# One head's tokens on all 128 partitions: a linear-attention and mixture-of-experts kernel with a new token layout

## The chip, the cores and the metric

The kernel runs on one core of a Trainium2 chip. The metric is the device time of one launch in microseconds (us). Three runs of the kernel before took 371.85, 367.94 and 371.0 us, median 371.0.

## The reference, cut to what matters

Linear attention (a cosine-weighted one) is followed by a top-1 mixture of experts on its output. All inputs are float32.

```
q, k, v: (B=8, H=8, S=576, D=64)
q_p, k_p = phi(x) = [relu(x)*cos(theta), relu(x)*sin(theta)]   # theta = pi/2 * position / S
kv  = einsum('bhsf,bhsd->bhfd', k_p, v);  z = sum_s k_p
num = q_p @ kv;  den = q_p . z + 1e-6;  x = num / den          # 4608 tokens of 512
logits = x @ w_gate;  expert = argmax(logits);  gate = softmax(logits)[expert]
out[i] = gate[i] * (relu(x[i] @ w1[expert]) @ w2[expert])      # 8 experts, 512 -> 1024 -> 512, capacity 1152
```

## The kernel before, in words

**Order of the work.** Every piece of work is registered with a planner (class `Plan`, lines 59 to 179): engine, cost in us, dependencies, buffers, a priority that the table `PHI` (line 28) shifts by kind. `schedule` runs a list schedule over these costs, and `emit` issues the instructions in the order of planned start. So each engine's queue is a fixed list; costs and `PHI` set its order, and on the chip each engine works through its list and waits at semaphores.

**Attention, batch by batch (8 batches).** Partition p holds head parity o = p // 64 and token group p % 64; each token group has 9 consecutive tokens j. A head therefore lies on 64 partitions, and two heads share the 128.

- `load` (L420 to L438): six DMAs a batch on SP's queue (v, k, v, k, q, q), 576 KB each, one DMA over all 128 partitions; a partition receives two runs of 9\*64 floats (2304 bytes).
- `scale_k`, `scale_v` (L448 to L467): per token j, k becomes relu(k)\*cos and a copy v\*tan is made, each 128x256 per instruction (128x128 in batch 0, split in two): 18 instructions a batch, on ACT or DVE as the planner chooses.
- `q_relu` (L480, tag reluq): one DVE instruction of 128x1152 per half batch, also reordering q; then `q_part` (L487): 9 TensorE transposes of 128x128 per half batch (L493) and three evictions from PSUM (L500).
- `kv_half` (L524, matmul at L535): k as stationary 64x64, v and v\*tan as moving 64x132; 9 j, two column halves c, two row halves o. The four combinations (o, c) are four 64x64 quarters of the array.
- Small steps that fold `w_gate` into kv: copy (L548), transpose (T, L559), product (G, L573), copy back (L579).
- `p_unit` (L595): num and den and logits of 128 tokens and four heads, 10 units a batch: four matmuls of 64 rows (L603), ACT copy (L613), DVE multiply-add (L617). Units rotate through three PSUM slots.

**Routing (L635 to L819).** DVE computes argmax, gate, and with small matmuls (`f_cnt`, L716) each token's rank within its expert; POOL scatters the token rows to a DRAM buffer `xd` sorted by expert (L796).

**Experts.** 43 blocks of 128 sorted rows (`block`, L969): fetch on SP's queue (L994) into one of four `xr` buffers, transpose (L1003), copy (L1007), up-projection in two halves m=0 and m=1 against w1 (L1023), relu (L1032/1034), transpose (L1041), copy (L1047), down-projection (L1067), copy (L1072), indirect store by POOL (L1081). The first 20 blocks ("a") can start when six batches are routed; the other 23 ("b") need all batches and the zero rows `s_pad` (L924 to L933), which fill each expert's last block: eight DMAs of 128.5 KB issued from ACT's queue.

**Weights.** POOL's queue loads w1 and w2 with a cast to bf16. w1's first half (w1a, L945) has its own place and loads between batches 4 and 7; the second half (w1b) and w2's first half live in a pool that takes the place of all attention buffers, so their loads wait for the operation `swap` (L1124), after the last attention batch; w2's second half takes w1a's place.

Of the kernel before, what the change touches and what calls it, by code (L numbers as in the profile page):

```python
# [20 lines left out]
P = 128  # L21
# [7 lines left out]
    "G": 0.31, "KV": 0.33, "P": 0.35, "Q": -0.14, "T": -0.36, "carry": 1.34, "count": -1.01, "down": 0.6,  # L29
    "end": -3.84, "fetch": 0.26, "gout": 1.98, "ix": 1.87, "kva": 0.07, "load": -0.87, "pad": -0.91,  # L30
    "pre": -0.09, "relu": -1.78, "reluq": -0.77, "rq": 8.8, "scat": -0.24, "seen": -0.1, "tab": 0.69,
    "tmp": 1.28, "tsb": 1.62, "turn": -1.07, "up": -0.52, "vt": 17.49, "w1": 1.81, "w2": 0.68, "warm": -0.07,
    "wg": -0.36, "xT": -5.44, "xturn": -10.62,
# [3 lines left out]
class Slots:  # L37


    def __init__(self, name, n, fifo=True):  # L40
        self.name, self.n, self.fifo = name, n, fifo
        self.holder = [None] * n
        self.vers, self.given = [], 0

# [14 lines left out]
class Plan:  # L59
# [30 lines left out]
    def schedule(self, window=0.25, switch=0.15, sticky=0.6):  # L90
# [11 lines left out]
        while done < len(self.ops):  # L102
            best = {}
            cands = []
            for o in ready:
                t = o.avail
                ok = True
                for v in o.vers:
                    if v.slot is not None:
                        t = max(t, v.ready)  # L110
                    else:
                        ts = []
                        for h in v.slots.holder:
                            if h is None:
                                ts.append(0.0)
                            elif all(u.start is not None for u in h.uses):
                                ts.append(max(u.end for u in h.uses))
                        if not ts or (v.slots.fifo and v.turn != v.slots.given):
                            ok = False
                            break  # L120
                        t = max(t, min(ts))
# [23 lines left out]
            for v in o.vers:  # L145
                if v.slot is None:
                    opts = []
                    for i, h in enumerate(v.slots.holder):
                        if h is None:
# [11 lines left out]
            if o.dma:  # L161
                dma_free = max(dma_free, o.end) + o.dma
                o.end = dma_free + 1.6
# [19 lines left out]
def kernel(  # L183
# [21 lines left out]
    assert J == 9  # L205
    NJ = J // 2
# [12 lines left out]
    U0, U1, U2 = 4, 41, 42  # L219
# [36 lines left out]
    qrS = Slots("qr", 2)  # L256
# [5 lines left out]
    xrS = Slots("xr", 4)  # L262
# [4 lines left out]
    VH = J * D + 2  # L267
    VX = D + 2
    v_t = [early.tile([P, HB * VH + HB * J * VX], FP32, name=f"v{i}") for i in range(vS.n)]

    def v_raw(slot):
        return v_t[slot][:, 0:HB * VH].rearrange("p (h x) -> p h x", h=HB)

    def v_tan(slot):
        return v_t[slot][:, HB * VH:].rearrange("p (h j x) -> p h j x", h=HB, j=J)
# [5 lines left out]
    nc.vector.memset(zrow[:], 0.0)  # L281

# [27 lines left out]
    tok_n = late.tile([P, J], FP32, name="tok_n")  # L310
    nc.vector.tensor_scalar(out=tok_n[:], in0=colf[:, 0:J], scalar1=p9[:], scalar2=float(math.pi / (2.0 * S)),
# [3 lines left out]
    cosn = const.tile([P, J], FP32, name="cosn")  # L315
    sinn = const.tile([P, J], FP32, name="sinn")
    nc.scalar.activation(out=sinn[:], in_=tok_n[:], func=ACT.Sin)
    nc.scalar.activation(out=cosn[:], in_=tok_n[:], func=ACT.Sin, bias=halfpi[:])
    tann = const.tile([P, J], FP32, name="tann")
# [9 lines left out]
    prow = const.tile([P, 1], FP32, name="prow")  # L329
    nc.vector.tensor_copy(out=prow[:], in_=prow_i[:])  # L330
    base9 = const.tile([P, 1], FP32, name="base9")
    nc.vector.tensor_scalar(out=base9[:], in0=prow[:], scalar1=float(D), scalar2=p9[:], op0=ALU.is_ge, op1=ALU.add)
    tok_f = late.tile([P, NC], FP32, name="tok_f")
    nc.vector.tensor_scalar(out=tok_f[:], in0=colf[:, 0:NC], scalar1=2.0, scalar2=base9[:], op0=ALU.mult, op1=ALU.add)
# [14 lines left out]
    for i in range(vS.n):  # L349
        nc.gpsimd.memset(v_tan(i)[:, :, :, D], 1.0)  # L350
        nc.gpsimd.tensor_copy(out=v_tan(i)[:, :, :, D + 1], in_=tann[:].unsqueeze(1).to_broadcast([P, HB, J]))
    for i in range(vS.n):
        nc.gpsimd.memset(v_raw(i)[:, :, VH - 2:VH], 0.0)
# [20 lines left out]
    mjj = const.tile([P, P], BF16, name="mjj")  # L374
# [14 lines left out]
    def count_1():  # L389
# [3 lines left out]
        nc.vector.tensor_scalar(out=mlt[:], in0=m64[:], scalar1=p64[:], scalar2=None, op0=ALU.is_gt)  # L393
        nc.vector.tensor_scalar(out=meq[:], in0=m64[:], scalar1=p64[:], scalar2=None, op0=ALU.is_equal)

    def count_2():
        nc.vector.memset(mjj[:], 0.0)
        nc.vector.tensor_copy(out=mjj[0:D, D:P], in_=meq[0:D, D:P])
        nc.vector.memset(mltt[:], 0.0)
        nc.vector.tensor_copy(out=mltt[0:D, :], in_=mlt[0:D, :])  # L400
# [19 lines left out]
    def load(b, name, u):  # L420
# [7 lines left out]
        src = srcs[name][b].rearrange("(u c o) (p j) d -> u (o p) c (j d)", u=2, o=2, j=J)[u]  # L428

        def f():  # L430
            if name == "v":
                m = v_raw(ver.slot)[:, 2 * u:2 * u + 2, 0:J * D]
            elif name == "k":
                m = tl(ver, [P, HB, J, D], FP32, "early")[:, 2 * u:2 * u + 2, :, :].rearrange("p c j d -> p c (j d)")
            else:
                m = tl(ver, [P, 2, J, D], FP32, "early")[:].rearrange("p c j d -> p c (j d)")
            nc.sync.dma_start(out=m, in_=src)
        op("SP", 0.5, f, w=[(name, b, u)], vers=[ver], prio=b - 1.2, dma=1.55).tag = ("load", name, b, u)  # L438
# [3 lines left out]
    def attention(b):  # L442
# [4 lines left out]

        def scale_k(j, us):  # L448
            def f(eng):
                kk = km.tile[:, 2 * us[0]:2 * us[-1] + 2, j, :]  # L450
                if eng == "ACT":
                    nc.scalar.activation(out=kk, in_=kk, func=ACT.Relu, scale=cosn[:, j:j + 1])  # L452
                else:
                    nc.vector.tensor_scalar(out=kk, in0=kk, scalar1=0.0, scalar2=cosn[:, j:j + 1], op0=ALU.max,
                                            op1=ALU.mult)
            return f

        def scale_v(j, us):
            def f(eng):
                heads = slice(2 * us[0], 2 * us[-1] + 2)  # L460
                dst, src = v_tan(vm.slot)[:, heads, j, 0:D], v_raw(vm.slot)[:, heads, j * D:(j + 1) * D]
                if eng == "ACT":
                    nc.scalar.activation(out=dst, in_=src, func=ACT.Copy, scale=tann[:, j:j + 1])  # L463
                else:
                    nc.vector.tensor_scalar(out=dst, in0=src, scalar1=tann[:, j:j + 1], scalar2=None,
                                            op0=ALU.mult)
            return f  # L467

        for us in ((0, 1),) if b else ((0,), (1,)):
            for j in range(J):  # L470
                less = 0.1 if not b else 0.0
                op("ACT", 0.4 - less, scale_k(j, us), r=[("k", b, u) for u in us], w=[("k1", b, j, u) for u in us],
                   vers=[km], prio=pr - 0.3 + 0.05 * us[0] + 0.01 * j, lat=0.14, alt=("DVE", 0.29 - less)).tag = ("k1", b, j)
                op("ACT", 0.4 - less, scale_v(j, us), r=[("v", b, u) for u in us], w=[("vt", b, j, u) for u in us],
                   vers=[vm], prio=pr - 0.3 + 0.05 * us[0] + 0.01 * j, lat=0.14, alt=("DVE", 0.29 - less)).tag = ("vt", b, j)
# [4 lines left out]
        def q_relu(u, qr):  # L480
            def f():
                t = tl(qr, [P, J, 2, D], FP32, "early")
                nc.vector.tensor_scalar(out=t[:].rearrange("p j c d -> p c j d"), in0=loaded[b, "q", u].tile[:],  # L483
                                        scalar1=0.0, scalar2=None, op0=ALU.max)
            return f

        def q_part(u, jq, pv, qr):  # L487
            js = range(4 * jq, min(4 * jq + 4, J))

            def f():  # L490
                q_ps = tl(pv, [P, 512], FP32, "ps")
                for n, j in enumerate(js):
                    nc.tensor.transpose(out=q_ps[:, n * P:(n + 1) * P],  # L493
                                        in_=qr.tile[:, j, :, :].rearrange("p c d -> p (c d)"), identity=ident[:])

            def g(eng):
                t = tl(rq[u], [P, 2, J * D], FP32, "early")
                n = len(js)
                col = 0 if jq == 2 else D + 4 * D * jq
                (nc.scalar.copy if eng == "ACT" else nc.vector.tensor_copy)(out=t[:, :, col:col + n * D].rearrange("x o (j p) -> x o j p", j=n),  # L500
                               in_=pv.tile[:, 0:n * P].rearrange("x (j o p) -> x o j p", j=n, o=2))
            return f, g

        for u in range(2):
            qr = Ver(qrS)
            op("DVE", 0.67, q_relu(u, qr), r=[("q", b, u)], w=[("qr", b, u)], vers=[loaded[b, "q", u], qr],
               prio=pr - 0.4).tag = ("reluq", b, u)
            for jq in range(3):
                pv = Ver(aS)
                f, g = q_part(u, jq, pv, qr)  # L510
                n = 4 if jq < 2 else 1
                op("PE", 0.13 * n, f, r=[("qr", b, u)], w=[("qps", b, u, jq)], vers=[pv, rq[u], qr], prio=pr,
                   lat=0.2, mode="full").tag = ("Q", b, u, jq)
# [10 lines left out]
        def kv_half(u):  # L524
            def f():
                kv_v = kv_tile()
                for j in range(J):
                    for c in range(2):
                        v0 = (2 * u + c) * VH + j * D
                        v1 = HB * VH + ((2 * u + c) * J + j) * VX  # L530
                        for o in range(2):
                            rows = slice(o * D, (o + 1) * D)
                            first = v_t[vm.slot][rows, v0:v0 + VX]
# [667 lines left out]
```

## Time and profile before

| what | us |
|---|---|
| median of three runs | 371.0 |
| the profiled execution's own time | 362.18 |
| its span, first to last instruction | 360.4 |
| first attention matmul (kv of batch 0) starts | 11.3 |
| kv of batches 1, 2, 3, 4 starts | 31.2, 50.3, 66.6, 82.5 |
| kv of batches 5, 6, 7 starts | 98.3, 115.3, 132.9 |
| last attention matmul (L603) ends | 150.7 |
| up-projections (L1023) run | 151.1 to 277.6 |
| down-projections (L1067) run | 278.0 to 352.6 |
| PE, DVE, ACT, POOL busy | 317.5, 187.3, 202.5, 126.9 |

The page splits the span into 40 slices and gives for every engine the busy share of each; below that come groups of instructions by source line with count, busy time (the union of their times) and mean duration of one, and the idle time of the engine ahead of them with what ended it. Matmuls are pipelined, so the mean duration of one is longer than the distance to the next; the rate is read from the busy time of an unbroken run divided by its count. A float32 matmul is recorded as two matmuls (two passes), a float32 transpose as one. PEld is the loading of stationary operands, which runs beside the matmuls.

### The profile page before, as it was taken

Reading aid. Unit: us, or ns where it says so; the run is one execution under the profiler, and the core shown is the slowest. Engines: PE = TensorE matmul, PEld = TensorE weight load, DVE = VectorE, ACT = ScalarE, POOL = GpSimd, SP = SyncE. Lnnn points to the kernel's source line nnn. Section 1 sums busy time; section 2 is a strip of 40 time slices with the busy share of each in tenths; the row PEclk is TensorE's granted clock in tenths of the full one; section 3 lists DMA queues with packets and bytes.
Section 4 is the critical chain, followed back from the end, with each engine's and each line's share of the span. In section 5 each row is a group of like instructions: output and inputs, shape, how many; then the busy total and the mean of one; then the engine's idle time right before and its main releaser. Section 6 shows DMA issues by size and latency. Waiting matters only on the chain.

```text
span 360.4 us, 9576 instructions
## 1 busy us (share of the span) xinstructions
PE 317.5 (88%) x3344; PEld 208.9 (58%) x3368; DVE 187.3 (52%) x546; ACT 202.5 (56%) x450; POOL 126.9 (35%) x189
## 2 busy tenths in 40 slices
PE   5779798999989998883998889999999999999991
PEld 1668687878778787642555445555555444444440
DVE  5777889888898888787374435443333000000000
ACT  3588898989698754643444444555554333333330
POOL 5000424252807252657223222320000455555552
PEclk9899899999999899996899999999999999999997
DMA  4999939596995768599999996499100244342230
GB/s 156 394 391 387 344 118 341 181 360 144 382 292 191 119 120 132 148 179 246 207 225 213 215 201 124 76 211 211 27 3 0 94 162 156 146 163 113 92 132 0
DMA packets 38542, 66.62 MB, mean 185 GB/s; under 512 B 3903, under 2 KB 18655, under 8 KB 38498
## 3 DMA queue, kind: packets, MB, share of 16 engines
q0 software_dynamic: 18096, 31.00, 39.6%
q1 hardware_dynamic: 19250, 33.98, 27.4%
q10 hardware_dynamic: 1152, 1.05, 1.1%
q8 instruction: 29, 0.48, 0.5%
q14 instruction: 15, 0.12, 0.1%
HBM read 67.56 MB, written 17.06 MB: 235 GB/s over the span
## 4 chain that ended last, share of the span: by engine, by line
PE 43%; DMA 16%; ACT 10%; DVE 10%; issue 9%; POOL 7%; SPq 2%; ACTq 1%; POOLq 1%; DVEq 0%
PE p L1023 18%; PE p L1067 10%; PE p L603 7%; POOL out_dram L1081 6%; DMA xr<-xd 6%; PE a L1041 5%; DMA v<-in_v_dram 4%; DMA km<-in_k_dram 3%; ACT km L452 3%; DVE num L617 3%; DVE xg L786 2%; ACT v L463 2%; DMA w1a<-in_moe_w_dram 2%; PE a L1003 2%; DMA xd<-zrow 1%
## 5 line engine op out<-in xcount | busy, mean ns | idle before, releaser
L1067 PE MATMUL p<-w,un 128*128 x337 | 74.2, 379 | 0.5 <-issue 0.2
L796 POOL DMA_INDIRECT xd<-xg,si x40 | 45.4, 1135 | 81.9 <-DVE xg L786 64.8
L1032 ACT ACTIVATE h<-p 128x512 bf16<-128x512 f32 x65 | 38.9, 598 | 35.0 <-PE p L1023 32.2
L1067 PEld LDWEIGHTS <-un 128*128 128x128 bf16 x344 | 33.6, 98 | 40.4 <-issue 0.5
L603 PE MATMUL p<-kva,rq 64*128 64x146 f32 x640 | 51.7, 305 | 2.3 <-DVE num L617 0.6
L1072 ACT COPY y<-p 128x512 f32<-128x512 f32 x42 | 24.6, 585 | 48.0 <-PE p L1067 46.9
L1047 DVE COPY un<-a 128x512 bf16<-128x512 bf16 x66 | 27.9, 423 | 43.0 <-PE a L1041 42.9
L603 PEld LDWEIGHTS p<-kva,rq 64*128 64x128 f32 x640 | 44.8, 196 | 8.3 <-DVE num L617 4.6
L1023 PEld LDWEIGHTS <-un 128*128 128x128 bf16 x344 | 32.3, 98 | 28.9 <-issue 6.8
L1023 PE MATMUL p<-w1a,un 128*128 x162 | 43.8, 390 | 2.9 <-issue 1.4
L617 DVE SCALAR_TENSOR_TENSOR num<-p,tant,tmp 128x292 f32<-128x292 f32 (+1 forms) x80 | 39.9, 519 | 11.3 <-ACT tmp L613 10.7
L1023 PE MATMUL p<-w1b,un 128*128 x165 | 43.1, 378 | 1.1 <-issue 0.8
L535 PE MATMUL p<-v,km 64*64 64x132 f32 x1152 | 36.0, 279 | 5.7 <-DMA v<-in_v_dram 4.8
L1081 POOL DMA_INDIRECT out_dram<-y,ids x20 | 19.6, 979 | 58.9 <-ACT un L1047 44.6
L535 PEld LDWEIGHTS p<-v,km 64*64 64x64 f32 x1152 | 33.8, 136 | 7.9 <-issue 7.5
L613 ACT COPY tmp<-p 128x292 f32<-128x292 f32 (+1 forms) x77 | 30.8, 401 | 12.8 <-PE p L603 7.4
L1041 PEld LDWEIGHTS <-h 128*128 128x128 bf16 x344 | 25.2, 99 | 17.7 <-ACT h L1032 3.1
L1041 PE MATMUL a<-identb,h 128*128 128x128 bf16 x344 | 31.8, 221 | 0.7 <-ACT un L1007 0.5
L452 ACT ACTIVATE km<-km,cosn 128x256 f32<-128x256 f32 (+1 forms) x67 | 27.9, 485 | 1.9 <-DMA km<-in_k_dram 1.9
L1081 POOL DMA_INDIRECT out_dram<-y,ix x23 | 22.3, 972 | 16.9 <-ACT y L1072 16.9
L493 PE MATMUL a<-ident,qr 128*128 128x128 f32 x144 | 24.5, 291 | 3.1 <-DVE qr L483 1.2
L998 POOL COPY ids<-xr 128x2 bf16<-128x2 bf16 x43 | 8.8, 214 | 51.7 <-DMA xr<-xd 51.4
(169 smaller groups left out, 345.3 us busy)
## 6 DMA issues: line engine op xcount, KB each, us to landing
v<-in_v_dram SPq DMA_DIRECT2D x16, 576.0 KB, 8.8
km<-in_k_dram SPq DMA_DIRECT2D x16, 576.0 KB, 7.2
qm<-in_q_dram SPq DMA_DIRECT2D x16, 576.0 KB, 9.2
w<-in_moe_w_dram POOLq DMA_DIRECT2D x16, 512.0 KB, 8.1
xr<-xd SPq DMA_DIRECT2D x43, 128.5 KB, 5.2
w1a<-in_moe_w_dram POOLq DMA_DIRECT2D x8, 512.0 KB, 6.0
w1b<-in_moe_w_dram POOLq DMA_DIRECT2D x8, 512.0 KB, 8.8
xd<-zrow ACTq DMA_DIRECT2D x8, 128.5 KB, 7.3
```

Of the source, the lines that this page charges most:

```text
L452: nc.scalar.activation(out=kk, in_=kk, func=ACT.Relu, scale=cosn[:, j:j + 1])
L535: nc.tensor.matmul(out=kv_v[c * D:(c + 1) * D, 2 * o + u, :, :], lhsT=km.tile[rows, 2 * u + c, j, :], rhs=both, start=(j == 0), stop=(j == ...
L603: nc.tensor.matmul(out=p_ps[:, a, o, 0:2 * KW], lhsT=rq[u].tile[a * D:(a + 1) * D, o, col:col + P], rhs=kva.tile[a * D:(a + 1) * D, 2 * o ...
L613: (nc.scalar.copy if eng == "ACT" else nc.vector.tensor_copy)(out=t[0:rows], in_=by_t(0))
L617: nc.vector.scalar_tensor_tensor(out=num.tile[0:rows, c, u * HB:(u + 1) * HB, :], in0=by_t(1), scalar=tant[0:rows, c:c + 1], in1=tmp.tile[ ...
L796: si = nc.gpsimd.indirect_dma_start(out=xd[:, :], out_offset=bass.IndirectOffsetOnAxis(ap=xg.si[0:rows, c:c + 1], axis=0), in_=xg.tile[0:r ...
L1023: nc.tensor.matmul(out=hp, lhsT=xv.tile[:, g, :], rhs=w1h[m][:, bass.ds(e1, 1), g, :], start=(g == 0), stop=(g == G - 1))
L1032: nc.scalar.activation(out=h[:], in_=src, func=ACT.Relu)
L1041: nc.tensor.transpose(out=t_ps[:, x * P:(x + 1) * P], in_=hvs[m].tile[:, x // 2, x % 2, :], identity=identb[:])
L1047: (nc.scalar.copy if eng == "ACT" else nc.vector.tensor_copy)(out=unit(hts[m])[:].rearrange("p f s -> p (f s)"), in_=tvs[m].tile[:].bitcas ...
L1067: nc.tensor.matmul(out=y_ps, lhsT=hts[x // G].tile[:, x % G, :], rhs=w2h[x // G][:, bass.ds(e2, 1), x % G, :], start=(x == 0), stop=(x == ...
L1081: oi = nc.gpsimd.indirect_dma_start(out=out[:, :], out_offset=bass.IndirectOffsetOnAxis(ap=idx, axis=0), in_=yv.tile[:], in_offset=None, b ...
```

## The change

1. **Layout.** A head's 576 tokens go onto all 128 partitions: partitions 0 to 63 take tokens 0 to 3 of each group of nine, partitions 64 to 127 tokens 4 to 8. So there are five columns j (`NC`), the last on the upper half only. A load becomes two DMAs, one per partition half, with runs of 1024 or 1280 bytes; scaling becomes 10 instructions a batch of 128x512; kv becomes 40 matmuls a batch of 128 rows, 64 columns, in two column halves of the array, in place of 72 in quarters.
2. **q.** The DVE instruction `q_relu` goes. The transposes become ordinary matmuls against the identity, 64 output columns each in the two column halves of the array (20 per half batch in place of 9), and the relu is done by the eviction from PSUM.
3. **Buffers.** A tile `big` of w1b's size holds the first k and v buffers during attention; w1b is loaded there after kv of batch 6, no longer after `swap`. w1a's loads are tied to q's loads of batches 1 to 6. w2's first half waits for w1b's loads and for later blocks than before. `xr` has 7 buffers in place of 4.
4. **Pads.** `s_pad` issues its eight DMAs from SP's queue.
5. **Counting.** `f_cnt` uses 17 small matmuls in place of 15 (the new order of tokens); the index constants follow the layout. The zero columns of v are set by DVE at the start, ahead of the rest of the setup, instead of by POOL (L353).
6. **Planner.** A new `PHI`, new costs, and buffers in turn take their fixed slot. Its costs for the new work: 1.4 us per kv half (2.15 before), 0.14 per pair of q matmuls (0.13 per transpose before), 0.85 of DMA time per half load (1.55 per whole load before).

```diff
-        src = srcs[name][b].rearrange("(u c o) (p j) d -> u (o p) c (j d)", u=2, o=2, j=J)[u]
-        op("SP", 0.5, f, w=[(name, b, u)], vers=[ver], prio=b - 1.2, dma=1.55).tag = ("load", name, b, u)
+        src = srcs[name][b, HB * u:HB * u + HB].rearrange("h (p j) d -> p h (j d)", j=J)
+        def f(o):
...
+                nc.sync.dma_start(out=m[o * D:(o + 1) * D, :, 0:n], in_=src[:, :, o * NJ * D:o * NJ * D + n])
+        for o in range(2):
+            op("SP", 0.6, f(o), w=[(name, b, u)], vers=[ver], prio=b - 1.2, dma=0.85).tag = ("load", name, b, u)
...
-                    nc.tensor.transpose(out=q_ps[:, n * P:(n + 1) * P],
-                                        in_=qr.tile[:, j, :, :].rearrange("p c d -> p (c d)"), identity=ident[:])
+                for n, (i, j) in enumerate(cols):
+                    for c in range(2):
+                        nc.tensor.matmul(out=q_ps[c * D:(c + 1) * D, n * w:(n + 1) * w],
+                                         lhsT=loaded[b, "q", u].tile[rows, 2 * c + i, j, :], rhs=ident[rows, rows],
+                                         start=True, stop=True)
...
+                    nc.scalar.activation(out=dst, in_=src, func=ACT.Relu)
...
-                for j in range(J):
-                    for c in range(2):
-                        for o in range(2):
-                            rows = slice(o * D, (o + 1) * D)
-                            nc.tensor.matmul(out=kv_v[c * D:(c + 1) * D, 2 * o + u, :, :],
-                                             lhsT=km.tile[rows, 2 * u + c, j, :], rhs=both,
+                for j in range(NC):
+                    for i in range(2):
+                        for c in range(2):
+                            h = 4 * u + 2 * c + i
+                            nc.tensor.matmul(out=kv_v[c * D:(c + 1) * D, 2 * i + u, :, :],
+                                             lhsT=km.tile[part(j), h, j, :], rhs=both,
...
-                zi = nc.scalar.dma_start(out=xd[bass.ds(r0, P), :], in_=zrow[:])
+                zi = nc.sync.dma_start(out=xd[bass.ds(r0, P), :], in_=zrow[:])
...
-                w1h[n] = pools["mid"].tile([P, E, G, FH], BF16, name="w1b")
+                assert all(loaded[b, x].slot for x in "kv")
+                w1h[n] = big[:].bitcast(BF16).rearrange("p (e g f) -> p e g f", e=E, g=G)
...
-        w1_load(0, e, e + 0.1, ops_of("KV", min(4 + e // 2, B - 1)))
+        w1_load(0, e, e + 0.1, ops_of("load", "q", 1 + 3 * e // 4, 1))
-        w1_load(1, e, 50.0 + e, [swapped])
+        w1_load(1, e, 50.0 + e, ops_of("KV", B - 2))
```

## The prediction

> **What bounds the kernel now.** I read the windows view first, cut by stage (columns: length, then busy time of PE, PEld, DVE, ACT, POOL with counts, granted TensorE clock, DMA share, GB/s).
>
> ```profile
> 8.00:41.00 33.00, 24.80 (x443) 21.54 (x443) 25.10 (x97) 25.88 (x68) 0.32 (x1) 0.95 1.04 383
> 67.00:99.00 32.00, 30.21 (x558) 25.94 (x554) 27.99 (x74) 27.73 (x74) 14.82 (x15) 1.00 0.81 268
> ...
> 158.00:168.00 10.00, 2.81 (x16) 1.34 (x17) 9.02 (x34) 0.68 (x3) 5.69 (x7) 0.81 1.12 256
> 168.00:180.00 12.00, 11.31 (x74) 6.67 (x75) 5.03 (x11) 6.88 (x13) 3.87 (x10) 0.73 1.10 200
> 180.00:230.00 50.00, 44.77 (x353) 25.95 (x358) 24.84 (x72) 22.69 (x40) 11.86 (x36) 1.00 0.95 187
> 230.00:277.00 47.00, 46.16 (x332) 26.45 (x338) 18.72 (x44) 25.06 (x43) 5.63 (x8) 1.00 0.50 90
> ```
>
> To 41 us the loads bound it (DMA share 1.04, 383 GB/s). From 67 to 99 three engines are nearly full: PE 30.2 of 32, DVE 28.0, ACT 27.7. A relief of DVE or ACT alone buys little there, and work added to PE is paid. At 158 to 168 PE has 2.8 us of work in 10, and half a clock after it. Later PE is full. The waits of that hole:
>
> ```profile
> ACT un L1007 <- DMA xd<-zrow: 9.3, 1, 9.3
> PE a L1003 <- DMA xd<-zrow: 7.0, 1, 7.0
> SPq L437 <- POOL v L353: 3.2, 1, 3.2
> ```
>
> ACT's timeline says why: its queue issues the eight pads, and its evictions stand behind them, so PE's PSUM slots stay full. The third line is the start: SP's first load waits until 3.89 us for POOL's memset.
>
> ```profile
> 158.85 8.44 ACTq L928 DMA_DIRECT2D xd<-zrow  x8
> 167.33 0.58 ACT L1007 COPY un<-a 128x512 bf16<-128x512 bf16 x1 [9.32 <-DMA xd<-zrow]
> ```
>
> Then the groups that the change touches, from the page:
>
> ```profile
> L603 PE MATMUL p<-kva,rq 64*128 64x146 f32 x640 | 51.7, 305 | 2.3 <-DVE num L617 0.6
> ...
> L535 PE MATMUL p<-v,km 64*64 64x132 f32 x1152 | 36.0, 279 | 5.7 <-DMA v<-in_v_dram 4.8
> ...
> L452 ACT ACTIVATE km<-km,cosn 128x256 f32<-128x256 f32 (+1 forms) x67 | 27.9, 485 | 1.9 <-DMA km<-in_k_dram 1.9
> ...
> L493 PE MATMUL a<-ident,qr 128*128 128x128 f32 x144 | 24.5, 291 | 3.1 <-DVE qr L483 1.2
> ```
>
> and one batch's kv from PE's timeline:
>
> ```profile
> 66.60 4.29 PE L535 MATMUL p<-v,km 64*64 64x132 f32 x144
> ```
>
> The counts: 576 kv matmuls make 1152 records, two passes each, while 144 q transposes make 144. The rate: (4.29 - 0.27) / 143 = 28 ns a record, so a slot of four quarters takes 112 ns. L603 has 24 records, 12 slots of two halves, in 1.78 us in the chain of waits: (1.78 - 0.28) / 12 = 125 ns.
>
> [...] No column-tiled, full-depth float32 matmul is in this trace. [...] The trace has 383 GB/s for loads over 128 partitions and none over 64.
>
> **The change part by part, per batch.**
>
> *kv on PE.* 72 matmuls x 2 passes / 4 quarters = 36 slots x 112.5 ns = 4.05 us. After: 40 x 2 / 2 = 40 slots, 4.50 us: **+0.45**. The full depth saves nothing, since the quarters filled the array already, and the fifth column is half empty.
>
> *q on PE.* Before: 8 transposes in 1.09 us elsewhere in the timeline, so about 0.11 each, 18 x 0.11 = 1.98. After: [...] 3.94, **+1.96**. [...]
>
> *DVE and ACT.* `q_relu` goes: 16 x 0.745 us (its group), -1.5 of DVE; the relu at eviction rides on a copy. Scaling: ACT's 128 columns take 390 ns and 256 take 499, so 512 about 717; DVE's 280 and 350 give 490. 18 instructions at 0.50 (9.0) become 10 at 0.72 (7.2): -1.8. Together 3.3 of about 29 us of both. PE gets back at most what it waits on them; at three nearly full engines I count 0.8 of its 2.4. Behind q's matmuls SP's next q load now waits for PE, not DVE; q has two batches of buffers, which cover it.
>
> *Loads.* 6 x 0.59 MB = 3.54 MB: at 383 GB/s 9.2 us, [...] I take 16.2. Scatters and w1a come on top: queue q0 takes 39.6% of 360.4 us for 31.0 MB, 4.6 us per MB; a batch's scatter (0.59 MB) is 2.7, w1a (4.2 MB over six batches) 3.2: 22 us if nothing overlaps, 16.2 if all does. The cover is two batches of k, v and q buffers and a PE period of 17.6 to 18.4; gone, PE waits for `km`, `v` and `qm`. SP issues twelve loads at about 0.46 us in place of six; hidden, as is `f_cnt` (two more small matmuls, records about 0.03 apart).
>
> *Start.* The first load moves from 3.89 to about 1.8 us. v and k of batch 1 are loads 7 to 10: 1.8 + 2.4 (first landing 7.79 - 3.89 - 1.5 of transfer) + 10 x 2.7 = 31.2; with scaling kv of batch 1 starts at 33.5, not 31.2.
>
> *Attention's end.* Steady periods are 16.0 (kv starts 50.3, 66.6, 82.5, 98.3). PE's would be 16.0 + 2.4 - 0.8 = 17.6, DMA's 16.2 to 22; I take 18.5. kv of batch 7 starts at 33.5 + 6 x 18.5 = 144.5. From there to the last P matmul is 17.8 now, about 19.3 then: 163.8 against 150.7, **+13**.
>
> *Pads.* Off ACT the hole goes: 7.05 us idle, and of the 12 us at clock 0.73 the equivalent of 3.2. On SP they take their 8.4 us ahead of later block fetches; PE needs about 1.3 us a block (L1003, L1023, L1041 at 0.056, 0.216, 0.056 each), so seven buffers cover 9 us, four only 5. I count **-7** (bounds: -10.3, and 0 if fetches starve PE). w1b earlier lets m=1 fill gaps in 180 to 230, where PE idles 5.2 us, some of it in evictions: 0 to -2, taken 0, since w1b shares the DMA with the last loads.
>
> *Sum.* +13 - 7 = **+6**. The profiled execution would go from 362.2 to 368. The median shown is 8.8 above that execution; I carry the difference over: 371 + 6 = **377**.
>
> **Rivals.**
> 1. *The forecast* (halved loads, heavier PE): 377, own range 368 to 392; the upper end is 22 us a batch of DMA for part of the batches. [...] Against: the kernel's planner books 0.85 us per half load, 1.70 for 1.55; a figure in source is no measurement. Chance 0.45.
> 2. *Loads hidden anyway*: the halves overlap, only PE pays. Period 17.6: kv of batch 7 at 31.5 + 105.6 = 137, attention ends at 156, +5.5; hole -8: 368 to 369, range 362 to 375. Chance 0.27.
> 3. *Faster*: [...] as the planner's 1.4 us per half and 0.14 per pair suppose. PE -1.6 a batch, and DVE and ACT 3.3 lighter: period about 14.3, 8 x -1.9 = -15, hole -10: 346. Against: both float32 rates above. It decides when a slot of two column halves takes under about 85 ns. Chance 0.20.
> 4. *The pads do not do what they are moved for*: SP's fetches stand behind them and PE idles as long. 377 + 7 = 384 to 390. Against: 7 buffers. Chance 0.08.
>
> **How the numbers follow.** About 1% (3.7 us) is what this kernel's measurement can tell from no change. Slower: most of 1 (0.36), little of 2 (0.06), all of 4 (0.08): 0.50. Same: 0.08 + 0.12 = 0.20. Faster: rival 3 (0.20), 0.01 of 1 and 0.09 of 2: 0.30. Range 350 to 394: below lies the lower half of rival 3, above the worst of 1 and 4.
>
> **What would show it.** Loads: GB/s while only loads run, [...] and their time to landing. kv: 80 records a batch, 56 ns or under 35 apart. q: records two per matmul. The hole: ACT without `xd<-zrow`, PE busy after routing of batch 7. kv of batch 7: near 144, 137 or 120. The prediction fails if loads keep over 330 GB/s and kv of batch 7 starts before 138.

## The result, and the profile after

The changed kernel took 407.7 us (median of four runs, 406.2 to 410.0) against 371.4 for the kernel before on the same chip: a ratio of 1.100, interval 1.090 to 1.110. Its profiled execution took 409.98 us, with a span of 408.2 (before 360.4) and a mean clock of 0.942. Chips differ: the kernel before took 362 to 365 us on some and 371 to 373 on others, so variants are compared by their ratio to it, taken on one chip. A second measurement of the changed kernel gave 1.097. The profiled execution of the kernel before (362.2) is quicker than any of its runs on the chip of the result (367.9 to 372.8). So the two profiles lie 47.8 us apart, while the medians differ by 36.3: what a table of the two profiles shows is some 11 us more than the change cost.

| us | before | after |
|---|---|---|
| kv of batches 1, 4, 7 starts | 31.2, 82.5, 132.9 | 49.8, 113.0, 167.5 |
| last attention matmul ends | 150.7 | 198.1 |
| rest of the span | 209.7 | 210.1 |

In these two profiles all of the loss lies in the attention; the experts' part is as long as before. The windows of the changed kernel, cut at its own stages (length, busy PE, PEld, DVE, ACT, POOL, granted clock, DMA share, GB/s):

```profile
16.00:50.00 34.00, 24.96 (x286) 22.13 (x288) 11.09 (x46) 13.08 (x30) 0.00 (x0) 0.80 1.14 215
...
73.00:113.00 40.00, 36.20 (x500) 30.80 (x498) 25.37 (x70) 24.35 (x54) 10.20 (x11) 0.94 1.06 209
199.00:207.00 8.00, 5.14 (x51) 3.00 (x50) 7.11 (x24) 3.99 (x9) 4.17 (x6) 1.00 0.45 124
207.00:216.00 9.00, 2.59 (x15) 1.25 (x16) 8.28 (x30) 2.37 (x4) 7.17 (x14) 0.90 0.44 142
216.00:270.00 54.00, 48.56 (x376) 29.63 (x383) 21.69 (x68) 27.00 (x48) 10.22 (x38) 0.92 0.69 140
270.00:325.00 55.00, 54.11 (x405) 31.57 (x411) 23.42 (x59) 27.94 (x47) 6.99 (x12) 1.00 0.58 107
```

The DMA engines are as full as they were in the first 41 us before (share over 1), but they move 209 to 215 GB/s, not 383, and they stay full through most of the attention. DVE and ACT, nearly full before, are over a third idle. The hole behind the last routing is still there, from about 199 to 216 us. The whole attention in one line, first the kernel before, then after:

```profile
0.00:150.70 150.70, 130.82 (x2162) 110.12 (x2163) 122.71 (x368) 114.86 (x297) 51.67 (x76) 0.97 0.81 249
```

```profile
0.00:198.10 198.10, 163.59 (x2153) 137.22 (x2154) 115.14 (x350) 101.21 (x227) 53.41 (x77) 0.91 1.04 208
```

198.1 us at 208 GB/s are 41.2 MB (37.5 before; w1b's 4.2 MB are now among them). On average DMA has no slack until kv of batch 7 starts at 167.5, and little after that. Two windows, cut there; the first holds the six periods from kv of batch 1 to kv of batch 7:

```profile
49.80:167.50 117.70, 105.52 (x1458) 89.50 (x1456) 76.28 (x202) 70.44 (x155) 32.97 (x35) 0.94 1.06 219
167.50:198.10 30.60, 28.22 (x404) 24.11 (x404) 22.49 (x71) 13.90 (x35) 13.68 (x18) 1.00 0.92 177
```

How a late load stops TensorE, which still has work: ACT's timeline in batch 1, and PE's beside it.

```profile
31.63 0.40 ACT L642 COPY tmp<-p 128x292 f32<-128x292 f32 x1 [0.57 <-PE p L632]
38.46 1.34 ACT L497 ACTIVATE v<-v,tann 128x512 f32<-128x512 f32 x2 [6.42 <-DMA big<-in_v_dram]
39.70 1.06 ACT L532 ACTIVATE rq<-a 128x512 f32<-128x512 f32 x2
```

```profile
33.67 1.97 PE L521 MATMUL a<-ident,qm 128*64 128x128 f32 x32 [0.22 <-DMA qm<-in_q_dram]
40.33 0.69 PE L521 MATMUL a<-ident,qm 64*64 64x64 f32 x8 [4.70 <-ACT rq L532]
```

ACT's next instruction scales v of batch 1 and waits 6.4 us for a load; DVE waits in the same way until 38.50. (The profile names the load into `big`, which was issued next to the last one of v; releasers are inferred.) Behind them stand the evictions of q (39.70) and of batch 0's P. So PE fills its PSUM slots by 35.6 and then idles 4.7 us: the profile puts this wait down to ACT's eviction and not to a load. After this stop the TensorE clock is at half for a stretch (0.66 on average from 40 to 50 us).

The groups that the change touches:

```profile
L632 PE MATMUL p<-kva,rq 64*128 64x146 f32 x640 | 57.4, 320 | 5.8 <-issue 2.5
...
L521 PE MATMUL a<-ident,qm 128*64 128x128 f32 (+1 forms) x640 | 44.1, 280 | 10.8 <-ACT rq L532 7.0
...
L564 PE MATMUL p<-big 128*64 128x132 f32 (+1 forms) x320 | 22.8, 297 | 10.0 <-DMA big<-in_v_dram 10.0
...
L532 ACT ACTIVATE rq<-a 128x512 f32<-128x512 f32 (+1 forms) x45 | 20.7, 484 | 14.2 <-PE a L521 13.8
```

q costs PE 44.1 us in place of 24.5 (640 records, two per matmul). L632 does the same matmuls as L603 before, in 57.4 us in place of 51.7. Most of that is the half clock: taken in windows of 2.5 us, the clock cost these matmuls 6.1 us, 2.4 before. SP's queue in the hole:

```profile
201.29 1.43 SPq L1028 DMA_DIRECT2D xr<-xd  x2
210.58 9.79 SPq L959 DMA_DIRECT2D xd<-zrow  x8
220.96 0.35 SPq L1028 DMA_DIRECT2D xr<-xd  x1
```

The pads are off ACT, but SP stands 7.6 us for the row that they need, which DVE writes after five copies of rows (its L817), and no block is fetched from 202.7 to 221.0.

### The profile page after: what moved, and what is told of

It is laid out like the page before. It is cut to its first block, busy times and chain, and to the rows that moved or that the text cites. A ratio compares the mean times of both kernels' runs of the same rounds, so it can differ in the third digit from the quotient of the medians.

```text
span 408.2 us, 9615 instructions
## 1 busy us (share of the span) xinstructions
PE 349.7 (86%) x3344; PEld 237.2 (58%) x3368; DVE 177.7 (44%) x533; ACT 189.2 (46%) x380; POOL 124.3 (30%) x187
## 4 chain that ended last, share of the span: by engine, by line
PE 51%; DMA 14%; issue 11%; POOL 6%; POOLq 6%; ACT 4%; SPq 3%; DVE 2%; another core or an unknown queue 1%; ACTq 0%; DVEq 0%
PE p L1057 17%; PE p L632 8%; PE p L564 8%; PE a L521 7%; DMA qm<-in_q_dram 6%; POOL out_dram L1115 6%; POOLq L1115 5%; PE a L1075 4%; DMA km<-in_k_dram 3%; DMA xr<-xd 3%; PE a L1037 2%; SPq L464 2%; DMA big<-in_v_dram 2%; PE a L602 2%; ACT rq L532 1%
## 5 line engine op out<-in xcount | busy, mean ns | idle before, releaser
L827 POOL DMA_INDIRECT xd<-xg,si x40 | 43.4, 1084 | 113.9 <-DVE xg L817 77.4
L1066 ACT ACTIVATE h<-p 128x512 bf16<-128x512 f32 x80 | 47.8, 598 | 54.8 <-PE a L1075 28.6
L632 PE MATMUL p<-kva,rq 64*128 64x146 f32 x640 | 57.4, 320 | 5.8 <-issue 2.5
L632 PEld LDWEIGHTS p<-kva,rq 64*128 64x128 f32 x640 | 48.2, 205 | 12.6 <-issue 6.4
L646 DVE SCALAR_TENSOR_TENSOR num<-p,tant,tmp 128x292 f32<-128x292 f32 (+1 forms) x80 | 38.9, 514 | 37.3 <-ACT tmp L642 30.6
L521 PE MATMUL a<-ident,qm 128*64 128x128 f32 (+1 forms) x640 | 44.1, 280 | 10.8 <-ACT rq L532 7.0
L521 PEld LDWEIGHTS a<-ident,qm 128*64 128x64 f32 (+1 forms) x640 | 35.1, 143 | 17.9 <-ACT rq L532 8.3
L1057 PE MATMUL p<-big,un 128*128 x164 | 42.9, 378 | 1.3 <-issue 0.7
L564 PE MATMUL p<-big 128*64 128x132 f32 (+1 forms) x320 | 22.8, 297 | 10.0 <-DMA big<-in_v_dram 10.0
L564 PEld LDWEIGHTS p<-big 128*64 128x64 f32 (+1 forms) x320 | 19.7, 147 | 13.2 <-issue 12.9
L532 ACT ACTIVATE rq<-a 128x512 f32<-128x512 f32 (+1 forms) x45 | 20.7, 484 | 14.2 <-PE a L521 13.8
```

The lines of the kernel that those rows point to most:

```text
L521: nc.tensor.matmul(out=q_ps[c * D:(c + 1) * D, n * w:(n + 1) * w], lhsT=loaded[b, "q", u].tile[rows, 2 * c + i, j, :], rhs=ident[rows, row ...
L564: nc.tensor.matmul(out=kv_v[c * D:(c + 1) * D, 2 * i + u, :, :], lhsT=km.tile[part(j), h, j, :], rhs=both, start=(j == 0), stop=(j == NC - 1))
L632: nc.tensor.matmul(out=p_ps[:, a, o, 0:2 * KW], lhsT=rq[u].tile[a * D:(a + 1) * D, o, col:col + P], rhs=kva.tile[a * D:(a + 1) * D, 2 * o ...
L646: nc.vector.scalar_tensor_tensor(out=num.tile[0:rows, c, u * HB:(u + 1) * HB, :], in0=by_t(1), scalar=tant[0:rows, c:c + 1], in1=tmp.tile[ ...
L827: si = nc.gpsimd.indirect_dma_start(out=xd[:, :], out_offset=bass.IndirectOffsetOnAxis(ap=xg.si[0:rows, c:c + 1], axis=0), in_=xg.tile[0:r ...
L1057: nc.tensor.matmul(out=hp, lhsT=xv.tile[:, g, :], rhs=w1h[m][:, bass.ds(e1, 1), g, :], start=(g == 0), stop=(g == G - 1))
```

## The experiments

To compare them I split the time from 5 us to the attention's end, in windows of 2.5 us, into PE's idle time (length less busy), time lost to the clock (busy time times 1 minus the granted clock) and the rest, PE's work at full clock.

The second column is the median of the kernel before on the chip of that row, in us; "rest" is the span after the attention.

| kernel | chip | ratio to before | attention ends | work | idle | clock | rest |
|---|---|---|---|---|---|---|---|
| before (its profile) | not known | 1 | 150.7 | 122.4 | 18.7 | 4.6 | 209.7 |
| after | 371 | 1.100 | 198.1 | 148.0 | 33.3 | 11.8 | 210.1 |
| after, second measurement | 372 | 1.097 | 199.0 | 147.2 | 31.2 | 15.6 | 206.1 |
| before, loads in partition halves | 362 | 1.113 | 191.5 | 119.8 | 43.6 | 23.1 | 211.4 |
| before, loads in heads | 363 | 0.999 | 149.2 | 122.8 | 18.2 | 3.2 | 212.2 |
| before, loads in even/odd partitions | 362 | 1.042 | 164.1 | 120.5 | 28.2 | 10.4 | 210.2 |
| before, two-pass matmuls for q | 362 | 1.027 | 159.3 | 137.5 | 15.1 | 1.7 | 210.4 |
| before, q's whole part | 364 | 1.054 | 157.8 | 137.6 | 10.9 | 4.3 | 223.0 |
| after, loads over 128 partitions | 363 | 1.016 | 168.9 | 146.4 | 14.4 | 3.1 | 199.0 |
| after, even/odd partitions | 363 | 1.048 | 174.4 | 139.6 | 27.9 | 1.9 | 198.3 |
| after, the planner's costs | 363 | 1.104 | 187.8 | 147.8 | 31.6 | 3.4 | 207.7 |
| after, pads on ACT's queue | 363 | 1.123 | 192.9 | 144.9 | 33.4 | 9.7 | 211.6 |
| after, the pads' row earlier | 363 | 1.086 | 188.8 | 145.0 | 28.2 | 10.7 | 200.9 |
| before, seven buffers, pads on SP | 363 | 0.973 | 151.2 | 121.0 | 18.4 | 6.8 | 201.7 |
| before, seven buffers, pads split | 372 | 0.975 | 158.3 | 124.2 | 27.6 | 1.5 | 200.9 |

**What the chip does to such a table.** The last two rows issue the same instructions in the same order on every engine up to the end of the attention; they differ in the pads behind it. On the chip of 363 the attention ends at 151.2 us, on the one of 372 at 158.3, with 9 us more of idle time on PE. The changed kernel shows the same: its two measurements on chips of 371 and 372 end the attention at 198.1 and 199.0. The two variants with other pads, whose order is the same up to there, end it at 192.9 and 188.8 on one chip of 363; that pair also shows how far two executions on one chip can differ, 4 us. So a row from a slower chip against one from a quicker chip overstates a loss in the attention by some 5 to 10 us. Why those chips are slower isn't shown.

**Loads alone in the kernel before.** Two DMAs a load, over partitions 0 to 63 and 64 to 127:

```diff
-            nc.sync.dma_start(out=m, in_=src)
+            for o in range(2):
+                nc.sync.dma_start(out=m[o * D:(o + 1) * D], in_=src[o * D:(o + 1) * D])
```

> The kernel before, each q, k or v load split into two DMAs by partition half (0 to 63, 64 to 127), same bytes and same runs of 2304 bytes. Theory L (loads over half the partitions run at half rate, and that is the main part of the loss): loads move 205 to 220 GB/s in the first 40 us instead of 383, the clock drops in the gaps, attention ends 10 to 25 us later than 150.7 and the time rises by 10 to 25 us. Theory P (the added work on TensorE alone is the loss, loads are hidden): under 3 us.

1.113 (1.099 to 1.127): the split of the loads alone costs as much as the whole change. Its window, in which the kernel before moved 390 GB/s:

```profile
20.00:30.00 10.00, 6.99 (x88) 5.55 (x80) 3.31 (x26) 4.03 (x10) 0.00 (x0) 1.00 1.06 227
```

**The same, even and odd partitions** (`m[o::2]`, `src[o::2]`).

> The kernel before, each load split into two DMAs of 64 partitions, the even and the odd ones; same number of DMAs, bytes and runs as the split by halves. If the reach of the partitions [...] sets the rate: about 380 GB/s as before and within 4 us of it. If a DMA of 64 partitions, or twice as many DMAs, is slow in itself: 205 to 220 GB/s and as slow as the split by halves.

1.042 (1.031 to 1.052), which neither theory had. The rate is whole again:

```profile
20.00:30.00 10.00, 8.07 (x98) 6.43 (x90) 5.71 (x29) 7.39 (x19) 0.00 (x0) 1.00 1.04 380
```

Yet the first kv starts at 14.5 us, not 11.3, and PE loses 9.5 us more to idling and 5.8 more to the clock.

**The same number of DMAs, all over 128 partitions:** one DMA for each head column (`m[:, c:c + 1]`).

> The kernel before with each of its 48 loads issued as two DMAs of 288 KB, one per head column, both over all 128 partitions: the number of DMAs of the even/odd run, but with every DMA spread over all partitions. Number theory (the even/odd run's loss of 4% is the price of twice as many DMAs on SP's queue, 0.6 us of issue each): as that run, ratio 1.03 to 1.05, first kv about 14.5 us, attention to about 162 us. Spread theory (its loss comes from half of the partitions in one DMA, even where they are every second one): ratio below 1.01, first kv at 11 to 12 us, attention to about 151 us.

0.999 (0.996 to 1.002), attention to 149.2 us. The number theory falls: twice as many DMAs on SP's queue cost nothing here. (Its first load started at 0.74 us, not 3.9, since it no longer waits for POOL's memset, and its first kv at 9.7; that lead of 1.6 us is the whole difference at the end, 1.5.) So it is the partitions that one DMA spans. Why every second partition still costs 4% isn't settled.

**Full-rate loads in the changed kernel.** The same number of DMAs, now 320 KB each (the change has 256 and 320), over all partitions, from rows at a uniform stride. So other tokens lie on a partition than the constants are for, and the output is not that of the reference; the work and its order on every engine stay:

```diff
-                nc.sync.dma_start(out=m[o * D:(o + 1) * D, :, 0:n], in_=src[:, :, o * NJ * D:o * NJ * D + n])
+                h0 = srcs[name][b, HB * u + 2 * o]
+                rows = bass.AP(h0.tensor, h0.offset, [(287, P), (S * D, 2), (1, NC * D)])
+                nc.sync.dma_start(out=m[:, 2 * o:2 * o + 2, 0:NC * D], in_=rows)
```

> The changed kernel with the same number of loads of 320 KB, but each over all 128 partitions and one pair of heads instead of over 64 partitions and four heads; the rows come from other tokens, so the attention is taken over wrong tokens, everything behind it is done in full. Load theory: 350 GB/s or more while loads run, attention ends near 150.7 + 19 of TensorE work = 170 us in place of 198, ratio 1.03 to 1.05. Order theory (the planner's order of TensorE and SP makes the waits, whatever the loads take): attention still ends after 185 us, ratio above 1.07.

1.016 (1.008 to 1.023), below the 1.03 to 1.05 of the load theory, since the rest of the span is shorter too; 374 GB/s from 20 to 40 us; attention ends at 168.9 where the load theory said 170:

```profile
0.00:168.90 168.90, 153.33 (x2152) 129.40 (x2153) 115.49 (x350) 101.69 (x227) 53.63 (x77) 0.97 0.95 261
```

PE has the same number of instructions as after (2152 and 2153). Its runs of 1280 bytes are hardly longer than the change's (1024 and 1280), and the split loads above kept runs of 2304; so it isn't the short runs that slow the loads. The 29.2 us by which the attention is shorter are idle time (18.9), clock (8.7) and work (1.6); but the two traces are from a chip of 371 and one of 363. Against the two variants with other pads on a chip of 363 (192.9 and 188.8) it is 24 and 20 us, and that is what the loads are seen to cost.

**The changed kernel with even and odd partitions:** lower and upper tokens of each group on even and odd partitions, constants and identity columns to match, loads `m[o::2]` of 320 KB.

> The changed kernel with the two token groups on even and odd partitions instead of the lower and upper half: the two DMAs of a load cover the even and the odd partitions, 1280 bytes each run (11% more bytes), the fifth column of k is zeroed by its cosine, the matmuls and all else stay. Theory L: loads at 330 GB/s or more, attention ends 20 to 30 us before 198, time 378 to 390. Theory P: loads do not matter, 402 to 408. Theory O (the order planned with too low costs is the loss): likewise above 400.

1.048 (1.033 to 1.063): about half of the loss comes back. Its setup delays the first load to 4.37 us and its first kv to 24.1, where most of its idle time lies.

**The planner's costs** (kv half 1.4 to 2.35, q pair 0.14 to 0.23, half load 0.85 to 1.4 us).

> The changed kernel, planned with costs near what its trace shows: 2.35 us per kv half (1.4), 0.23 per pair of q matmuls (0.14), 1.4 us of DMA per half load (0.85). Only the order of the queues changes. Theory O: 10 us or more faster than 407.7. Theories L and P: within 6 us of it.

1.104 (1.093 to 1.116): no difference from the changed kernel that the intervals show. Attention ends at 187.8, which is 1 and 5 us before the two variants with other pads on the same chip. The order theory, which asked for 10 us or more, falls.

**q's matmuls.** First only two-pass matmuls against the identity in place of the transposes, in the kernel before:

```diff
-                    nc.tensor.transpose(out=q_ps[:, n * P:(n + 1) * P],
-                                        in_=qr.tile[:, j, :, :].rearrange("p c d -> p (c d)"), identity=ident[:])
+                    nc.tensor.matmul(out=q_ps[:, n * P:(n + 1) * P],
+                                     lhsT=qr.tile[:, j, :, :].rearrange("p c d -> p (c d)"), rhs=ident[:],
+                                     start=True, stop=True)
```

> The kernel before with q's 144 transposes made by ordinary float32 matmuls against the identity: 288 records, 18 x 0.109 = 2.0 us more on TensorE a batch, about what the new q matmuls add; nothing else changes, the planned order neither. Theory P: nearly all is paid, plus 12 to 16 us. Theory L: TensorE waits of 10 to 15 us in attention take part of it up, plus 5 to 11 us.

1.027 (1.014 to 1.039), attention to 159.3 us, PE's work +15.1: 1.9 a batch. Then q's whole part, with `q_relu` gone, 64-column matmuls and relu at eviction:

> The kernel before with the change's way for q alone: no relu of q ahead on VectorE, 18 matmuls of 64 columns per half batch against the identity in the two column halves (36 two-pass float32 matmuls in place of 18 one-pass transposes a batch), relu at the eviction; loads, scaling, kv, buffers and pads as before. TensorE theory (the forecast's step of about 2 us a batch stands and VectorE's relief hides): attention ends at 157 to 163 us in place of 150.7, ratio 1.015 to 1.03, near the run with two-pass matmuls in place of the transposes (1.027). Relief theory (1.34 us of VectorE a batch given up are on the path): attention ends at 149 to 155 us, ratio 0.99 to 1.01.

Attention to 157.8, as the TensorE theory has it: work +15.2. Against the matmuls alone, DVE's relief brings 1.5 us at most, by one execution of each. But the ratio is 1.054 (1.045 to 1.063), beyond both theories, since the rest of the span grew by 13. The windows and ACT's timeline of that kernel:

```profile
170.00:180.00 10.00, 0.00 (x0) 0.10 (x1) 6.61 (x27) 0.29 (x1) 5.52 (x10) 0.69 1.00 224
180.00:190.00 10.00, 8.56 (x47) 4.96 (x48) 2.39 (x5) 5.22 (x10) 2.10 (x5) 0.63 0.98 174
```

```profile
167.15 12.53 ACTq L932 DMA_DIRECT2D xd<-zrow  x8
179.71 0.58 ACT L1051 COPY un<-a 128x512 bf16<-128x512 bf16 x1 [13.06 <-DMA xd<-zrow]
```

The replanned order puts the pads where they hold ACT for 12.5 us in place of 8.4, and PE is empty for 10. An edit in the attention moved a stall of the experts' part.

**Pads.** On SP's queue in the kernel before (three lines in `s_pad`: SP for ACT):

> The kernel before with the eight pads issued from SP's queue instead of ACT's, all else as before (the planner places them anew). As the prediction's step had it: the hole of 7 us at 160 to 168 and the half clock after it go, minus 7 (to minus 10) us. If the hole only moves, because block fetches stand behind the pads in SP's queue: within 3 us.

1.004 (1.001 to 1.008). Nothing is gained:

```profile
160.00:170.00 10.00, 9.53 (x73) 5.38 (x72) 9.00 (x34) 8.72 (x18) 6.90 (x11) 1.00 1.09 235
170.00:180.00 10.00, 6.65 (x44) 3.70 (x45) 2.31 (x5) 3.96 (x8) 2.77 (x7) 0.83 1.11 195
180.00:190.00 10.00, 8.71 (x63) 4.59 (x64) 2.62 (x7) 5.15 (x10) 2.58 (x8) 1.00 1.13 223
190.00:200.00 10.00, 7.75 (x65) 4.58 (x64) 4.05 (x14) 4.41 (x8) 3.13 (x8) 1.00 1.14 222
```

The hole at 160 is gone and comes back in parts from 170 to 200: SP issues the pads from 160.04 to 166.88, the next fetch only at 167.67, and four buffers hold no more.

In the changed kernel, pads back on ACT's queue, and apart from it DVE's row for the pads moved ahead of its copies (`PHI` "end" to -40):

> The changed kernel with the pads back on ACT's queue. If the move to SP gave its gain and the loss lies elsewhere: 6 to 10 us slower than 407.7. If the move gave nothing: within 3 us.

> The changed kernel with one entry of the priority table moved (end: -1.11 to -40), so that DVE makes the pads' row numbers right after the last batch's counts, ahead of five row copies of 3.1 us. If SP's wait for them (7.6 us) and the block fetches behind are what keeps the hole open: minus 3 to minus 8 us. If the hole has another cause: within 2 us.

1.123 (1.110 to 1.136) and 1.086 (1.075 to 1.096). Both intervals overlap one of the changed kernel's two (1.090 to 1.110, 1.081 to 1.113), so neither effect is shown. The rest of the span was 211.6 and 200.9 us.

**Row buffers.** Seven `xr` buffers in the kernel before (two fewer `un` in one pool and two more in the next make the room), once with pads on SP, once on ACT:

```diff
-    xrS = Slots("xr", 4)
+    xrS = Slots("xr", 7)
```

> The kernel before with pads on SP's queue (as one run before it, which gained nothing) and also seven row buffers for the experts instead of four, as the change has. Theory H (the hole behind the last batch's routing only moved to SP's queue since four buffers cannot bridge eight pads; seven bridge it): attention ends at 150 to 153 us, the rest takes 198 to 202 us as in the interleaved variant, in place of 209.7; span 350 to 354, ratio 0.97 to 0.98. Rival (the hole waits for the scatters of the last batch and not for the pads): ratio 0.995 to 1.005.

> The kernel before with pads left on ACT's queue and seven row buffers instead of four. Theory H: the hole is ACT waiting in its pads while its copies stand behind them, which more buffers do not mend: ratio 0.99 to 1.00, the hole at 160 us stays. Rival (buffers alone are what was missing, the queue of the pads does not matter): as the run with pads on SP and seven buffers, 0.97 to 0.98.

0.973 (0.964 to 0.982) and 0.977 (0.970 to 0.983), with the rest of the span at 201.7 and 204.8 us. Both beat both kernels, and the pads' queue makes no difference that the intervals show: theory H was wrong about the reason. With pads on ACT the hole stays, and the gain lies behind it:

```profile
160.00:170.00 10.00, 3.21 (x18) 1.97 (x18) 6.75 (x27) 3.15 (x6) 7.03 (x13) 0.70 1.13 252
180.00:190.00 10.00, 6.80 (x45) 3.87 (x45) 4.61 (x13) 2.34 (x4) 2.78 (x9) 0.83 1.15 228
190.00:200.00 10.00, 9.74 (x90) 6.24 (x89) 8.01 (x22) 4.33 (x8) 2.58 (x9) 1.00 1.08 207
200.00:210.00 10.00, 9.82 (x84) 6.13 (x86) 7.69 (x24) 4.10 (x8) 3.39 (x10) 1.00 1.08 216
210.00:220.00 10.00, 9.87 (x90) 6.43 (x91) 7.40 (x18) 4.96 (x9) 2.01 (x6) 1.00 0.86 144
```

From 190 on PE is busy 9.7 to 9.9 of 10 us. With four buffers it was less:

```profile
190.00:200.00 10.00, 8.99 (x73) 5.25 (x72) 5.09 (x16) 4.62 (x8) 2.99 (x8) 1.00 1.09 212
200.00:210.00 10.00, 8.31 (x70) 4.81 (x69) 3.84 (x12) 4.86 (x9) 2.62 (x8) 1.00 1.12 217
210.00:220.00 10.00, 8.94 (x66) 4.86 (x67) 4.60 (x15) 4.18 (x8) 2.24 (x8) 1.00 0.84 167
```

With four, SP's fetches waited 39.9 us in all for transposes to free an `xr`, with seven 20.1. In 180 to 230 the profile of before had shown this, as PE's missing 5.2 us in 50.

With pads split, four on SP and four on ACT:

> The kernel before with seven row buffers and four pads on SP's, four on ACT's queue. If what is left of the hole (PE busy 3.9 of 10 us with all pads on SP, 3.2 with all on ACT) is eight issues of 0.9 us in one queue: rest after attention 198 to 200 us in place of 201.7, ratio 0.965 to 0.97. If it is the scatters and weight loads that the next rows wait for: as with pads on SP, 0.97 to 0.98.

0.975 (0.963 to 0.988), the rest 200.9: no better than all on SP. (Its attention ended at 158.3 us, on the chip of 372.) With q's whole part added to pads on SP and seven buffers:

> As the kernel before with pads on SP's queue and seven row buffers (0.973), and the change's way for q as well. TensorE theory: 0.985 to 1.00, worse than without. Relief theory: 0.965 to 0.98.

1.002 (0.999 to 1.006): q's part takes 3% from that version too.

**The changed kernel again**, to see how much belonged to one execution:

> The changed kernel itself once more, on the chip of its variants. Theory of the chip (the variants with the end row earlier, pads on ACT's queue or other planner costs differ from the changed kernel by less than the attention's end differs from one execution to another): attention ends at 187 to 195 us in place of 198.1, the span is 395 to 402, the ratio stays at 1.09 to 1.11. Theory of the order (the variant with an earlier end row ended attention 9 us earlier for a reason in its order): attention ends at 196 to 200 us again. For the experts' part: if ACT's copies behind the last routing again start 1 to 4 us after what they wait for, it takes 208 to 212 us; if that belonged to one execution, 199 to 202.

Attention to 199.0 us, ratio 1.097: on such a chip the end at 198 to 199 is no accident of one execution. The rest took 206.1, between the two guesses, and ACT's copies again start late in the hole (205.98, 207.42, 208.90, 214.67). But this chip ran the kernel before in 372 us and the chip of the variants in 363, so the run doesn't decide between its two theories. The traces do: up to the end of the attention the two variants with other pads issue the same instructions in the same order, so order can't be why they ended it 5 to 10 us earlier.

## Why the prediction was wrong, step by step

The direction was right, and so was the mechanism of the likeliest case, halved loads (227 GB/s over one half of the partitions, 390 over all, in the kernel before); the time was 31 us too low, outside the range.

- **Loads: right.** That loads over one half of the partitions would be slower, 16.2 us a batch, was not shown by any trace when the forecast was made; it was the author's estimate. 204 to 216 GB/s was measured from 20 to 60 us (238 in the ten before). Full loads, half loads and heads (390, 227, 390 GB/s in the same window of the kernel before) show that it is the partitions of one DMA.
- **Attention's end: this is the step that failed.** It said 163.8, the trace has 198.1. All three terms of its sum were too small: kv of batch 1 starts at 49.8 and not 33.5 (16.3 us), the six periods after it take 19.6 us each and not 18.5 (6.7 in all), and from kv of batch 7 to the last P matmul it takes 30.6 and not 19.3 (11.3). In the two variants with other pads, on a chip of 363, the start is at 50.6 and 49.5, the period 18.8 and 18.4, the tail 29.2 in both. So start and tail failed on either kind of chip; the period was near.
  - *The start* is the largest term. v of batch 1 is in at 38.5 us and k's scaling starts at 41.5, where the forecast had the loads in at 31.2 (k's last half load is the 23rd on SP's queue, 11.5 loads in place of the 10 counted); then scaling, q's evictions and P, which had stood behind the load, share ACT and DVE, and kv starts 8 us after k's first scaling. The step had a term for the transfer, and none for PE's idling behind ACT and DVE, which stand in line for a load with evictions behind them, nor for half clock after it.
  - *The period* is DMA's: 219 GB/s over 117.7 us are 25.8 MB, 4.3 MB a period, with a DMA share of 1.06. The same bytes take 18.8 and 18.4 us in the two variants, at 226 and 234 GB/s. So PE's 17.6 was not the bound, as the step said. But its 18.5 was a middle between 16.2 and 22, not a sum of bytes, and that it came so near is luck.
  - *The tail* is not the loads': with full-rate loads it is 29.2 us (139.7 to 168.9). In both, kv of batches 6 and 7 start within 8 us of each other, and q and P of both come after. The forecast kept the old order here (17.8) and added 1.5.
- **What the loads are worth:** by ratios, 1.100 to 1.016. In the attention they are 20 to 24 us on chips alike (29.2 between the two traces above); the rest of the ratio is a shorter span behind the attention (199.0, and 201 to 212 in the three variants on such a chip with half loads), whose cause isn't settled. 18.2 us of attention stay with full-rate loads.
- **kv and q on PE: right in kind, together too small.** For q the forecast holds: its work is +1.9 us a batch (1.96 forecast). That its matmuls would take two passes was the author's estimate; 640 records for 320 matmuls show it. The time of a slot follows from the trace of before: 112 ns for 132 columns and 125 for 146 are some 0.85 ns a column, an estimate of 109 for 128. kv takes 5.17 us for 80 records with full-rate loads, some 62 ns apart where 56 was said; its groups sum to 43.0 us there, 36.0 before: +0.9 a batch where +0.45 was said. In all PE's work grew by 24 to 26 us, not 19. Rival 3 is out: a slot of two halves takes about 110 ns for q and 124 for kv, where it needed under 85.
- **DVE and ACT:** busy 21.2 us less in the attention, 2.7 a batch (3.3 forecast). That PE gets back 0.8 a batch came out by luck: q's whole part added 15.2 us of work and 7.1 to the attention, so 8.1 came back, 1.0 a batch. But 6.5 of it came back with the two-pass matmuls alone (15.1 of work, 8.6 later), without any relief of DVE: PE's idle time shrank.
- **Pads: wrong.** -7 was counted, the rest of the span is +0.4. In the kernel before the move alone is worth nothing (1.004) and seven buffers alone 2.3%. The reason given, that seven buffers cover the pads, was half right: with seven buffers the rest is 199.0 in the changed kernel with full loads. That it is the buffers and not the pads' queue is shown for the kernel before alone. Rival 4 came true in the changed kernel, beside rival 1 and not in place of it. Why that hole lasts while the same order with full loads has none isn't settled: ACT's copies start 1.4 to 5.3 us after the recorded end of the matmuls that they wait for.
- **Rival 2** (loads hidden) forecast an end at 156; with full loads it is 168.9. PE's work grew by 24.0 us there, not 19, and only 5.8 came back as less idle time and clock.

So with full-rate loads 8.4 of the 10% go, part of them behind the attention. The 1.6 that stay with full-rate loads are 18.2 us more in the attention less 10.7 in the rest, the gain of seven buffers. In the changed kernel as it is, that gain is spent again in the hole.

## What to carry to other kernels

Before a layout change, ask which partitions one DMA covers (here 390 GB/s over all 128, 380 over every second one, 227 over one half), and add up all bytes of a period at the rate that is left: where that sum exceeded the engines' period, it was the period here (4.3 MB at 219 GB/s, 19.6 us), whatever DVE and ACT gained. Price a late load by what stands behind the instruction that waits for it: here the engines' fixed order carried its wait to evictions, to PSUM and to PE. Before two traces are subtracted, see that their chips agree on an unchanged kernel: here that was worth 5 to 10 us of attention. And where a change bundles parts, look for the one that pays alone: here three more row buffers, worth 2.3 to 2.7% in the kernel before.

## What was not expected of the hardware

- A load split into even and odd partitions moved 371 to 400 GB/s from 10 to 30 us, as one over all 128 does, while a split into lower and upper half moved 227 from 20 to 30. All the same it cost 4% of the time.
- Twice as many DMAs of half the size, over all partitions, cost nothing (0.999).
- The granted clock was 0.5 in stretches of 3.4 to 13.7 us, many of them after a stop of PE: in the changed kernel PE idled 4.7 us up to 40.3, and the clock was 0.50 to 0.51 from 40 to 45 us. In the kernel with split loads half clock cost 23.1 us of PE's time, against 4.6 before, beside 43.6 us of idle time (18.7 before), so the stops of that kernel cost more than their length. A stop has no fixed price: with the planner's other costs PE idled 31.6 us and lost only 3.4 to the clock.
